# Gate and up projection in seven products per pair of tiles, with streamed down weights

## The chip, the cores and the metric

The kernel runs on one core of one Trainium2 chip. The metric is the device time of one execution in microseconds (us), as the median of several runs. The profiled execution is a separate one; its span goes from the first to the last instruction of the core.

## The reference, cut to what matters

```python
mod = silu(c) @ w_mod                       # six vectors sa, ca, ga, sb, cb, gb of 1024
h = layernorm(x) * (1 + ca) + sa
x = x + ga * attention(h)                   # 32 heads, window of 512 keys, wq [1024, 4096], wo [4096, 1024]
h = layernorm(x) * (1 + cb) + sb
g = silu(h @ w_gate)                        # w_gate, w_up: [1024, 3584]
u = h @ w_up
x = x + gb * ((g * u) @ w_down)             # w_down: [3584, 1024]
```

There are 2048 tokens of 1024 numbers, all bf16. The change is in the last four lines, the feed-forward part.

## The kernel before, in words

A token chunk is 512 tokens, and there are four of them. Tokens lie along the free dimension of the normed input `h_sb[slot]`, which has eight tiles of 128 input features by 512 tokens; slot is the chunk's number modulo 2. The residual `x_sb` stays in SBUF for the whole kernel.

The program runs in this order: opening (conditioning vectors, first layer norm), attention for chunks 0 to 3 of 32 heads each, every chunk followed by its output projection `oproj`, and then the feed-forward part for chunks 0 to 3. The order on each engine is the order in which the Python code emits the instructions; there is no scheduler. A tracker (`T.op`) puts a semaphore wait ahead of an instruction for each buffer that it reads or writes. Small generators in the list `tasks` (layer norm of a later chunk, conditioning vectors) are advanced one step at a time by `run()`, which the main loops call between their own instructions. All bulk transfers are issued by the SP engine, in program order, so a transfer that waits holds up those behind it.

The query projection of the attention already uses seven products instead of eight for a pair of 128-wide heads by two blocks of 256 tokens (`product`, `snap`, `q_add`); its sums of weights (`weight_sums`, L541) and of inputs (`input_sums`) are in fp16.

The feed-forward part before, for each chunk:

- `gateup(ch, ft)` for 28 feature tiles `ft` of 128 columns: 8 matmuls of 128x512 into a gate bank and 8 into an up bank (two banks each, in turn). ScalarE takes tanh(g/2) from the gate bank (L981), VectorE multiplies (t+1)*g (L982) and then times 0.5*u (L984) into `gu`.
- `down(ch, tt, lo, n)` for four token tiles by two halves of the output: 28 matmuls of 128x512 into one of four banks, then `add_to_x` multiplies by the gate vector (L680), adds to `x_sb` (L682), and the row of 128 tokens is stored.

Gate and up weights are loaded in groups of 512 columns (1 MB each, three groups in SBUF), for each chunk anew. The down weights are loaded once, in four parts, and stay. The layer norm of chunk 0 (`ln2[0]`) runs as a task during the attention of chunk 3, the layer norm of chunk n+1 during `gateup` of chunk n.

`oproj(3)` has 256 matmuls of 128x512; 16 of them are done inside the last four heads, then come 48, then 4 blocks of 32, each of which needs one load `load_wo` of 1 MB, then 8 groups of 8 with `add_to_x` behind each.

Of the kernel before, what the change touches and what calls it, by code (L numbers as in the profile page):

```python
# [3 lines left out]
ALU = mybir.AluOpType  # L4
# [4 lines left out]
P = 128  # L9
# [109 lines left out]
def bass_adaLN_cond__sliding_block_cached__swiglu_ffn__prompt_kernel(  # L119
# [28 lines left out]
    FG = FT // 4  # L148
# [104 lines left out]
    Q_last = [dq("q_last%d" % i) for i in range(3)]  # L253
# [6 lines left out]
    with nc.Block() as block:  # L260

        @block.gpsimd
        def _(g):
# [569 lines left out]
            for i in range(NA):  # L833
# [88 lines left out]
            NWG = 3  # L922
            G_AT = [(AT_WQ, AT_WQ + 8), (AT_TQ, AT_TQ + 8), (AT_MS, AT_MS + 8)]
            B_wg, B_wu, wg, wu = [None] * NWG, [None] * NWG, [None] * NWG, [None] * NWG
            Q_wg = [dq("q_wg%d" % i) for i in range(NWG)]
            Q_wu = [dq("q_wu%d" % i) for i in range(NWG)]

            def take_group(s):
                B_wg[s], B_wu[s] = _Buf("wg%d" % s), _Buf("wu%d" % s)
                wg[s] = M.take(G_AT[s][0] * KB, [DT, 512], BF16, [B_wg[s]])  # L930
                wu[s] = M.take(G_AT[s][1] * KB, [DT, 512], BF16, [B_wu[s]])

            def load_gu(gi):
                if gi >= NCH * FG:
                    return
                fg, s = gi % FG, gi % NWG
                for q_, dst, src, b_ in ((Q_wg[s], wg[s], B_w_gate, B_wg[s]), (Q_wu[s], wu[s], B_w_up, B_wu[s])):
                    T.op(q_, lambda: SP.dma_start(dst, src[:, fg * 512:(fg + 1) * 512].rearrange("(k p) n -> p k n", p=P)),
                         writes=[b_])

            take_group(0)
            take_group(1)
            steps = [lambda: None, lambda: load_gu(0), lambda: load_gu(1)]

            def each():
                run(2)
                if steps:
                    steps.pop(0)()

            oproj(NCH - 1, o_list[o_done:], each)  # L950
            finish(ln2[0])
            take_group(2)
            load_gu(2)
            NWD = 4
            B_wd = bufs("wd", NWD)
            wd = M.take(AT_WO * KB, [FT, D], BF16, B_wd)
            Q_wd = [dq("q_wd%d" % i) for i in range(NWD)]
            FW_ = FT // NWD

            def load_wd(i):  # L960
                T.op(Q_wd[i], lambda: SP.dma_start(
                    wd[:, i * FW_:(i + 1) * FW_, :],
                    B_w_down[i * FW_ * P:(i + 1) * FW_ * P, :].rearrange("(f d) n -> d f n", d=P)), writes=[B_wd[i]])

            B_gu = bufs("gu", FT)
            gu = M.take(AT_KT * KB, [FT, CH], BF16, B_gu)
            B_th, B_t1 = bufs("th", 2), bufs("t1", 2)
            th = [M.take((AT_S + i) * KB, [CH], BF16, [B_th[i]]) for i in range(2)]
            t1 = [M.take((AT_S + 2 + i) * KB, [CH], BF16, [B_t1[i]]) for i in range(2)]

            def gateup(ch, ft):
                s = (ch * FG + ft // 4) % NWG
                ff = ft % 4
                gb_, ub_ = ft % 2, 2 + ft % 2
                hs = ch % 2
                for w_, b_, bb in ((wg[s], B_wg[s], gb_), (wu[s], B_wu[s], ub_)):
# [77 lines left out]
```

## Time and profile before

| | us |
|---|---|
| median of 3 runs | 1260.23 (1259.8 to 1261.22) |
| profiled execution, whole | 1259.42 |
| its span | 1257.6 |
| TensorE matmul busy | 1243.1 (99%) |
| VectorE busy | 612.6 (49%) |
| ScalarE busy | 379.0 (30%) |
| feed-forward part, start to the end of the span | about 674.7 to 1257.6 |

The granted TensorE clock is 1.000 of full speed over the whole span. The profile page gives busy time by engine, 40 slices of the span, transfers by queue, the chain of work that ended last, and the costliest groups of instructions by line. An engine's idle time is listed with what released it. Matmul ends are modelled, so the pace of matmuls is read from the distance between what waits for them, or from windows, and not from the mean duration of one.

### The profile page before, as it was taken

How to read it: one execution, taken by the hardware profiler on the slowest of the kernel's cores; microseconds unless marked ns; L12 is line 12 of the kernel's file. 1: busy time of each engine (PE TensorE's matmuls, PEld its weight loads, DVE VectorE, ACT ScalarE, POOL GpSimd, SP SyncE). 2: the span in 40 equal slices, each digit the busy share in tenths (PEclk: the TensorE clock that was granted, in tenths of full speed). 3: DMA queues.
4: the chain of work that ended last, by engine and by line, in shares of the span. 5: the costliest groups of instructions: out<-in, count | busy, mean ns of one | idle time of the engine just before them, and what ended most of it. 6: DMA issues, size and time to landing. Idle time of an engine off the chain costs nothing.

```text
span 1257.6 us, 20341 instructions
## 1 busy us (share of the span) xinstructions
PE 1243.1 (99%) x8298; PEld 709.7 (56%) x8298; DVE 612.6 (49%) x1272; ACT 379.0 (30%) x524; POOL 20.0 (2%) x41
## 2 busy tenths in 40 slices
PE   7999999999999999999999999999999999999999
PEld 4677547876467774688644444444444444444444
DVE  4988318884078860577405543155422543133321
ACT  4677305664046750376500110011100111011100
POOL 1000000000000000000000000000000000000000
PEclk9999999999999999999999999999999999999999
DMA  9999647996469974389267954047420664024200
GB/s 303 255 269 262 215 172 190 269 298 188 149 176 237 260 190 164 95 241 262 50 234 229 338 169 139 20 103 203 139 82 19 161 184 157 25 77 134 67 9 26
DMA packets 235997, 212.49 MB, mean 169 GB/s; under 512 B 106880, under 2 KB 206080, under 8 KB 232064
## 3 DMA queue, kind: packets, MB, share of 16 engines
q1 hardware_dynamic: 235888, 211.19, 59.2%
q8 instruction: 65, 1.06, 0.4%
q14 instruction: 28, 0.23, 0.1%
q10 hardware_dynamic: 16, 0.00, 0.0%
HBM read 174.07 MB, written 12.58 MB: 148 GB/s over the span
## 4 chain that ended last, share of the span: by engine, by line
PE 96%; DVE 1%; SPq 1%; DMA 1%; issue 1%; ACT 0%
PE ps L265 96%; DMA arena<-in_w_mod_dram 1%; SPq L284 1%; DVE arena L670 0%; DVE arena L746 0%; ACT arena L763 0%; DVE arena L602 0%; DMA arena<-arena 0%; DVE arena L636 0%; DVE arena L669 0%; SPq L275 0%; SPq L299 0%; PE ps L269 0%; DVE arena L354 0%; DVE arena L541 0%
## 5 line engine op out<-in xcount | busy, mean ns | idle before, releaser
L265 PE MATMUL ps<-arena 128*128 128x512 bf16 (+4 forms) x8249 | 1239.8, 312 | 8.2 <-DMA arena<-in_w_mod_dram 4.0
L265 PEld LDWEIGHTS ps<-arena 128*128 128x128 bf16 (+1 forms) x8249 | 706.4, 98 | 541.0 <-issue 9.9
L653 ACT ACTIVATE arena<-ps 128x1024 bf16<-128x1024 f32 x256 | 249.7, 1022 | 39.4 <-PE ps L265 36.4
L981 ACT ACTIVATE arena<-ps 128x512 bf16<-128x512 f32 x112 | 66.9, 597 | 518.0 <-PE ps L265 518.0
L680 DVE TENSOR_TENSOR arena<-ps,arena 128x512 bf16<-128x512 f32 (+1 forms) x65 | 44.4, 683 | 339.0 <-PE ps L265 339.0
L982 DVE SCALAR_TENSOR_TENSOR arena<-arena,ps 128x512 bf16<-128x512 bf16 x112 | 76.9, 687 | 141.4 <-ACT arena L981 141.4
L596 ACT ACTIVATE arena<-ps 128x256 f32<-128x256 f32 x134 | 51.3, 383 | 251.4 <-PE ps L265 250.6
L984 DVE SCALAR_TENSOR_TENSOR arena<-arena,ps 128x512 bf16<-128x512 bf16 x112 | 76.9, 687 | 54.5 <-PE ps L265 54.5
L670 DVE TENSOR_TENSOR arena<-ps,arena 128x512 bf16<-128x512 f32 x128 | 88.5, 691 | 4.7 <-DVE arena L669 0.2
L602 DVE TENSOR_TENSOR arena<-ps,arena 128x256 bf16<-128x256 f32 x180 | 75.5, 420 | 11.0 <-PE ps L265 6.3
L669 DVE RECIPROCAL arena<-ps 128x4 f32<-128x4 f32 x128 | 23.0, 180 | 43.3 <-PE ps L265 42.6
L746 DVE SCALAR_TENSOR_TENSOR arena<-arena 128x512 f32<-128x512 bf16 x56 | 41.5, 742 | 0.1
L354 DVE BATCH_NORM_STATS2 arena<-arena 128x6 f32<-128x512 bf16 x60 | 41.1, 685 | 0.1
L361 POOL TENSOR_TENSOR arena<-arena 128x1 f32<-128x1 f32 x30 | 17.5, 583 | 983.4 <-DVE arena L359 980.9
L541 DVE TENSOR_TENSOR arena<-arena 128x1024 f16<-128x1024 bf16 (+1 forms) x48 | 32.4, 682 | 0.2
L636 DVE CAST arena<-ps 128x256 bf16<-128x256 f32 x60 | 25.2, 419 | 10.2 <-PE ps L265 9.0
L682 DVE TENSOR_TENSOR arena<-arena 128x512 bf16<-128x512 bf16 (+1 forms) x65 | 27.3, 420 | 2.2
L598 DVE COPY arena<-ps 128x256 f32<-128x256 f32 x46 | 19.4, 421 | 13.8 <-PE ps L265 13.7
L375 DVE TENSOR_SCALAR arena<-arena 128x512 bf16<-128x512 bf16 x56 | 20.4, 405 | 0.0
L365 DVE TENSOR_SCALAR arena<-arena 128x1024 bf16<-128x1024 bf16 x32 | 17.3, 541 | 2.8 <-DMA arena<-arena 2.5
L269 PE MATMUL ps<-arena 128*128 128x128 bf16 (+1 forms) x49 | 4.9, 262 | 3.6 <-DVE arena L345 3.6
L358 DVE BATCH_NORM_AGGREGATE arena<-arena 128x2 f32<-128x12 f32 x30 | 6.3, 209 | 1.0
(43 smaller groups left out, 51.2 us busy)
## 6 DMA issues: line engine op xcount, KB each, us to landing
arena<-in_A_wq_dram SPq DMA_DIRECT2D x64, 512.0 KB, 4.9
arena<-in_A_wo_dram SPq DMA_DIRECT2D x32, 1024.0 KB, 5.5
arena<-in_B_w_gate_dram SPq DMA_DIRECT2D x28, 1024.0 KB, 5.3
arena<-in_B_w_up_dram SPq DMA_DIRECT2D x28, 1024.0 KB, 7.3
arena<-wq_sums SPq DMA_DIRECT2D x22, 1024.0 KB, 6.3
arena<-in_w_mod_dram SPq DMA_DIRECT2D x8, 1024.0 KB, 7.8
wq_sums<-arena SPq DMA_DIRECT2D x8, 1024.0 KB, 5.6
arena<-in_B_w_down_dram SPq DMA_DIRECT2D x4, 1792.0 KB, 10.5
```

What stands on the lines that cost most here:

```text
L265: T.op(PE, lambda: TE.matmul(out_ap, lhsT, rhs, start=start, stop=stop, skip_group_check=loose), reads=reads, writes=bb)
L354: T.op(DVE, lambda: V.bn_stats(st_sb[i][:, 6 * hf:6 * hf + 6], x_sb[:, t, 512 * hf:512 * hf + 512]), reads=[BX[t]], writes=[B_st[i]])
L541: T.op(st, lambda: e.tensor_tensor(dst, x, y, op), reads=reads, writes=[dst_b])
L596: T.op(ACT, lambda: A.activation(sn[k], bank(QBK, 256), AF.Copy), writes=PB[QBK] + [B_sn[k]])
L602: T.op(DVE, lambda: V.tensor_tensor(dst, bank(XBK, 256, off), sn[k], ALU.add), reads=[B_sn[k]], writes=PB[XBK] + [B_q[i % NQ]])
L653: T.op(ACT, lambda: A.activation(ex[i % NEX][:, kt:kt + 2, :], bank(SCB[kt], 1024).rearrange("p (a b) -> p a b", a=2), AF.Exp, scale=att_s ...
L670: T.op(DVE, lambda: V.tensor_tensor(o_sb[i % NOS].rearrange("p (a b) -> p a b", a=TPC), num, rl_bc, ALU.mult), reads=[B_rl], writes=both + ...
L680: T.op(DVE, lambda: V.tensor_tensor(rt[s][:, 0:n], ps_ap, gate[:, lo:lo + n], ALU.mult), reads=[gate_b], writes=bb + [B_rt[s]])
L746: T.op(DVE, lambda: V.scalar_tensor_tensor(acc, ms[:, kc, :], sc[:, kc:kc + 1], acc, op0=ALU.mult, op1=ALU.add), reads=[B_ms, B_sc, B_acc] ...
L981: T.op(ACT, lambda: A.activation(th[e], bank(gb_), AF.Tanh, scale=0.5), writes=PB[gb_] + [B_th[e]])
L982: T.op(DVE, lambda: V.scalar_tensor_tensor(out=t1[e], in0=th[e], scalar=1.0, in1=bank(gb_), op0=ALU.add, op1=ALU.mult), reads=[B_th[e]], w ...
L984: T.op(DVE, lambda: V.scalar_tensor_tensor(out=gu[:, ft, :], in0=t1[e], scalar=0.5, in1=bank(ub_), op0=ALU.mult, op1=ALU.mult), reads=[B_t ...
```

## The change

Two chunks are taken together as a stretch of 1024 tokens, so the feed-forward part has two stretches. For a pair of feature tiles (256 columns) and a stretch, the weight block is split 2x2 (input features 0 to 511 and 512 to 1023, left and right 128 columns), and the input block 2x2 (input features, first and second chunk). Seven products of 4 matmuls of 128x512 give the four result blocks, in place of 4 blocks of 8 matmuls (Strassen's method in Winograd's form). This holds for gate and for up, so a pair has 14 products, 56 matmuls, in place of 64.

- `sums_of_pair`: VectorE forms four sums of 128x512 of the weights of the next pair, for gate and up, in fp16.
- `stretch_sums`: VectorE forms four sums of the inputs of a stretch, each in two instructions of 128x1024.
- `keep`: products 1, 6 and 5 accumulate in one bank (one for gate, one for up); after each of them ScalarE copies the running total to SBUF in fp32.
- `add`: products 2, 7 and 4 go to banks of their own (4 onto 7), and VectorE adds the kept total to each.
- `silu` on ScalarE uses the Silu function in place of Tanh; `times` multiplies on VectorE, one instruction for each of the four result blocks.
- Weights of a pair are loaded as two transfers of 512 KB (`load_raw`, rows of 512 bytes), three pairs in SBUF.
- `down` runs once for each half of the output and each stretch, with eight banks for eight token tiles at once. Its weights come in blocks of 4 feature tiles by 512 columns (512 KB), six or seven in SBUF, 28 blocks for the two stretches and two halves (one of them twice).
- The layer norm of chunk 1 moves to the end of the attention of chunk 3 and into `oproj(3)`; those of chunks 2 and 3 move into the two down passes of stretch 0. `oproj` calls `each()` also between its first 48 matmuls, which emits the first two weight loads, the Silu table load, the rest of the layer norm and the sums.

```diff
                 for n, a_ in enumerate(first):
                     o_mm(*a_)
+                    if n % 4 == 3:
+                        each()
...
+                if ch == NCH - 1 and h == 28:
+                    finish(ln2[0])
+                    ln2[1] = ln_task(1, g2, B_g2, sb, B_sb)
+                    tasks.append(ln2[1])
...
+            def pair_product(gp, m, n, b):
+                w_, bw = raw[gp % NRW][m], B_raw[gp % NRW][m]
+                ti = (2 * gp + m) % NTS
+                s_i = {3: 3, 5: 0, 6: 1, 7: 2}.get(n)
+                t_i = {4: 3, 5: 0, 6: 1, 7: 2}.get(n)
+                for kc in range(4):
...
+                    mm(bank(b), lhsT, rhs, kc == 0 and n in (1, 2, 7), kc == 3, [lb, hb], PB[b], loose=True)
...
+                def keep(m, n, i):
+                    b = acc_b[m]
+                    pair_product(gp, m, n, b)
+                    T.op(ACT, lambda: A.activation(fn[m][i], bank(b), AF.Copy), writes=PB[b] + [B_fn[m][i]])
+
+                def add(m, n, b, i):
+                    pair_product(gp, m, n, b)
...
+                    T.op(DVE, lambda: V.tensor_tensor(ring[c_], bank(b), fn[m][i], ALU.add),
+                         reads=[B_fn[m][i]], writes=PB[b] + [bs[c_]])
...
+                keep(0, 1, 0)
+                sums_of_pair(gp + 1, 0, 0)
+                g_ = add(0, 2, one[0], 0)
+                keep(1, 1, 0)
+                sl = silu(g_[0], [g_[1]], [])
+                keep(0, 6, 1)
+                sums_of_pair(gp + 1, 0, 1)
+                u_ = add(1, 2, one[1], 0)
+                times(f0, 0, u_, sl)
+                keep(1, 6, 1)
+                sums_of_pair(gp + 1, 0, 2)
+                keep(0, 5, 0)
+                sums_of_pair(gp + 1, 0, 3)
+                g_ = add(0, 7, two[0], 0)
+                keep(1, 5, 0)
+                sl = silu(g_[0], [g_[1]], [])
+                sums_of_pair(gp + 1, 1, 0)
+                u_ = add(1, 7, two[1], 0)
+                times(f1, 1, u_, sl)
+                pair_product(gp, 0, 3, acc_b[0])
+                sl = silu(bank(acc_b[0]), [], PB[acc_b[0]])
+                sums_of_pair(gp + 1, 1, 1)
+                g_ = add(0, 4, two[0], 1)
+                pair_product(gp, 1, 3, acc_b[1])
+                times(f1, 0, (bank(acc_b[1]),), sl, PB[acc_b[1]])
+                sl = silu(g_[0], [g_[1]], [])
+                sums_of_pair(gp + 1, 1, 2)
+                u_ = add(1, 4, two[1], 1)
+                times(f0, 1, u_, sl)
+                sums_of_pair(gp + 1, 1, 3)
+                load_raw(gp + NRW)
...
+                for b_ in range(2):
+                    for k in range(TPS):
+                        for f in range(4 * b_, 4 * b_ + 4):
+                            d_mm(k, f)
+                        each()
+                    load_wd(base + b_ + NWD)
+                for b_ in range(2, FG - 2):
+                    for f in range(4 * b_, 4 * b_ + 4):
+                        for k in range(TPS):
+                            d_mm(k, f)
+                        each()
+                    load_wd(base + b_ + NWD)
+                for k in range(TPS):
+                    for f in range(FT - 8, FT):
+                        d_mm(k, f)
...
+                    done(k, order[k], 0, n, Q_out[k % 4])
+                    each()
```

On ScalarE, the end of the attention and the feed-forward part read as follows before (L653 is the exponential of the attention, L596 a copy of the query projection, L981 the tanh of a feature tile):

```order
L596 ACTIVATE arena<-ps 128x256
L653 ACTIVATE arena<-ps 128x1024 x2
L596 ACTIVATE arena<-ps 128x256
L653 ACTIVATE arena<-ps 128x1024 x8
L981 ACTIVATE arena<-ps 128x512 x112
```

and now (line numbers are those of the changed kernel: L652 is the exponential, L1113 the first use of Silu, L996 the copy in `keep`, L1010 the `silu`):

```order
L652 ACTIVATE arena<-ps 128x1024 x8
L1113 ACT_TABLE_LOAD
L1113 ACTIVATE arena<-arena 128x4
L996 ACTIVATE arena<-ps 128x512 x2
L1010 ACTIVATE arena<-arena 128x512
L996 ACTIVATE arena<-ps 128x512 x4
L1010 ACTIVATE arena<-arena 128x512
L1010 ACTIVATE arena<-ps 128x512
L1010 ACTIVATE arena<-arena 128x512
L996 ACTIVATE arena<-ps 128x512 x2
```

One instruction for a feature tile and chunk has become ten for a pair of tiles and a stretch, six copies and four Silu; the row of the table load stands once.

On VectorE, two feature tiles of chunk 0 read before (L982 and L984 are the two products, L354 to L359 the layer norm of chunk 1):

```order
L354 BN_STATS arena<-arena 128x6
L982 SCALAR_TENSOR_TENSOR arena<-arena,ps 128x512
L984 SCALAR_TENSOR_TENSOR arena<-arena,ps 128x512
L354 BN_STATS arena<-arena 128x6
L358 BN_AGGR arena<-arena 128x2
L359 TENSOR_SCALAR arena<-arena 128x1
```

and the first part of a pair reads now (L540 is a sum of weights, L1003 the `add` from a bank, L1014 the `times`):

```order
L540 TENSOR_TENSOR arena<-arena 128x512
L1003 TENSOR_TENSOR arena<-ps,arena 128x512
L540 TENSOR_TENSOR arena<-arena 128x512
L1003 TENSOR_TENSOR arena<-ps,arena 128x512
L1014 TENSOR_TENSOR arena<-arena 128x512
L540 TENSOR_TENSOR arena<-arena 128x512 x2
L1003 TENSOR_TENSOR arena<-ps,arena 128x512
L540 TENSOR_TENSOR arena<-arena 128x512
L1003 TENSOR_TENSOR arena<-ps,arena 128x512
L1014 TENSOR_TENSOR arena<-arena 128x512
```

The layer norm is gone from between them, and sums of weights stand in its place, ahead of the additions that free the banks.

On SP, behind the last transpose of an attention head (L676), the transfers of `oproj(3)` read before (L503 is a block of `wo`, L938 a group of gate or up weights):

```order
L676 DMA_TRANSPOSE arena<-arena 128x4x128 [waits q_tr3,s_dve]
L503 DMA arena<-in_A_wo_dram 128x4x1024 [waits s_pe,q_wo0]
L503 DMA arena<-in_A_wo_dram 128x4x1024 [waits s_pe,q_wo1]
L503 DMA arena<-in_A_wo_dram 128x4x1024 [waits s_pe,q_wo2]
L503 DMA arena<-in_A_wo_dram 128x4x1024 [waits s_pe,q_wo0]
L938 DMA arena<-in_B_w_gate_dram 128x8x512 [waits q_wq0_1,q_wq0_0]
```

and now (L675 is the head's transpose, L946 `load_raw`, L370 the transposes of the layer norm of chunk 1, L502 `wo`):

```order
L675 DMA_TRANSPOSE arena<-arena 128x4x128 [waits q_tr3,s_dve]
L946 DMA arena<-in_B_w_gate_dram 128x8x256 [waits q_ms1]
L946 DMA arena<-in_B_w_up_dram 128x8x256
L946 DMA arena<-in_B_w_gate_dram 128x8x256 [waits q_ms0]
L946 DMA arena<-in_B_w_up_dram 128x8x256
L370 DMA_TRANSPOSE arena<-arena 128x8x128 [waits s_pe,q_tr0]
L370 DMA_TRANSPOSE arena<-arena 128x8x128 [waits q_tr1,s_dve]
L502 DMA arena<-in_A_wo_dram 128x4x1024 [waits s_pe,q_wo0]
L370 DMA_TRANSPOSE arena<-arena 128x8x128 [waits q_tr2,s_dve]
L370 DMA_TRANSPOSE arena<-arena 128x8x128 [waits q_tr3,s_dve]
L502 DMA arena<-in_A_wo_dram 128x4x1024 [waits s_pe,q_wo1]
```

Four weight loads and two transposes have moved ahead of the first block of `wo`, and two more transposes ahead of the second.

More of the change, by code (lines that the diff above doesn't have):

```diff
@@ L252, in bass_adaLN_cond__sliding_block_cached__swiglu_ffn__prompt_kernel @@
     Q_out = [dq("q_out%d" % i) for i in range(4)]
-    Q_last = [dq("q_last%d" % i) for i in range(3)]
+    Q_last = [dq("q_last%d" % i) for i in range(1)]
     tr_n = [0]
@@ L945, in each @@
[L945 to L963, printed above, removed]
@@ L987, in _ @@
[L987 to L997 removed]
+            NST, NPR, TPS = 2, FT // 2, 2 * TPC
@@ new lines, in _, with each @@
+            warm_s, B_ws = shift, B_shift
+            todo = prepare(True)
+            def each():
+                if len(todo) > 17:
+                    todo.pop(0)()
+                    return
+                for _ in range(2):
+                    if tasks:
+                        run()
+                    elif todo:
+                        todo.pop(0)()
+            oproj(NCH - 1, o_list[o_done:], each)
+            for g_ in list(tasks):
+                finish(g_)
+            while todo:
+                todo.pop(0)()
```

201 lines of the change are left out of this document (131 added, 70 removed).

## The prediction

> **What bounds the kernel now.** I read the page first (busy time, then the chain that ended last), and then the windows of the feed-forward part.
>
> ```profile
> PE 1243.1 (99%) x8298; PEld 709.7 (56%) x8298; DVE 612.6 (49%) x1272; ACT 379.0 (30%) x524; POOL 20.0 (2%) x41
> ...
> PE 96%; DVE 1%; SPq 1%; DMA 1%; issue 1%; ACT 0%
> ```
>
> TensorE is busy for 99% of the span and is 96% of the chain. The windows (length, busy time and instruction count of PE, PEld, DVE, ACT, POOL, then clock, DMA share, GB/s) show gate and up of chunk 0, its down projection, and gate and up of chunk 3:
>
> ```profile
> 674.70:771.30 96.60, 96.60 (x450) 43.81 (x448) 49.60 (x85) 16.72 (x28) 2.19 (x4) 1.00 0.70 219
> 771.30:819.60 48.30, 48.30 (x226) 21.88 (x225) 8.50 (x15) 0.00 (x0) 0.00 (x0) 1.00 0.17 58
> ...
> 1109.50:1206.00 96.50, 96.50 (x449) 43.78 (x448) 38.76 (x57) 16.72 (x28) 0.00 (x0) 1.00 0.28 90
> ```
>
> TensorE never idles there, at full clock, and the other engines are half idle. So in these stages time is the number of matmuls times their pace. The timeline of ScalarE gives the pace, since each tanh waits for its gate bank:
>
> ```profile
> 676.47 0.60 ACT L981 ACTIVATE arena<-ps 128x512 bf16<-128x512 f32 x1 [55.95 <-PE ps L265]
> 679.92 0.60 ACT L981 ACTIVATE arena<-ps 128x512 bf16<-128x512 f32 x1 [2.86 <-PE ps L265]
> ```
>
> 16 matmuls in 3.45 us are 0.2156 us each. The windows agree: 96.6/448 in groups of 8 to a bank, and 48.3/224 in groups of 28. Group length thus costs nothing, and I carry the pace over to groups of 4.
>
> **Part 1: fewer matmuls, -48.3 us.** Gate and up take 28 tiles x 4 chunks x 16 = 1792 matmuls before, and 14 pairs x 2 stretches x 56 = 1568 now. The 224 that go are worth 224 x 0.2156 = 48.3 us, if fp16 weights run at the same pace. Two groups of 256-wide matmuls in the query projection show that they do (busy, mean ns):
>
> ```profile
> L265 PE MATMUL ps<-arena 128*128 128x256 f16 x960 | 134.6, 273 | 0.1
> L265 PE MATMUL ps<-arena 128*128 128x256 bf16 x776 | 107.9, 273 | 2.4 <-ACT arena L763 1.2 <-DVE arena L636 0.6 <-DVE arena L669 0.3
> ```
>
> 134.6/960 = 0.140 us and 107.9/776 = 0.139 us. A pair then takes 56 x 0.2156 = 12.08 us, or 0.863 us for each of its 14 products, as long as the other engines keep up. The down projection keeps its 896 matmuls and its two 256-wide groups at the end, so nothing changes there.
>
> **Part 2: do VectorE and ScalarE keep up? 0 us.** Groups by form, whose durations I use:
>
> ```profile
> L602 DVE TENSOR_TENSOR arena<-ps,arena 128x256 bf16<-128x256 f32 x180 | 75.5, 420 | 11.0 <-PE ps L265 6.3
> L680 DVE TENSOR_TENSOR arena<-ps,arena 128x512 bf16<-128x512 f32 x63 | 43.5, 691 | 334.7 <-PE ps L265 334.7
> L680 DVE TENSOR_TENSOR arena<-ps,arena 128x256 bf16<-128x256 f32 x2 | 0.8, 424 | 4.2 <-PE ps L265 4.2
> L682 DVE TENSOR_TENSOR arena<-arena 128x512 bf16<-128x512 bf16 x63 | 26.7, 424 | 2.1
> L541 DVE TENSOR_TENSOR arena<-arena 128x1024 f16<-128x1024 bf16 x44 | 29.6, 681 | 0.0
> L541 DVE TENSOR_TENSOR arena<-arena 128x1024 f16<-128x1024 f16 x4 | 2.8, 692 | 0.1
> L981 ACT ACTIVATE arena<-ps 128x512 bf16<-128x512 f32 x112 | 66.9, 597 | 518.0 <-PE ps L265 518.0
> L481 ACT ACTIVATE arena<-arena 128x512 bf16<-128x512 bf16 x2 | 1.3, 715 | 1.0 <-DVE arena L419 1.0
> L342 ACT ACT_TABLE_LOAD x1 | 1.3, 1283 | 1.4 <-PEq L1039 1.4
> ```
>
> VectorE for a pair: 6 additions from a bank at 0.691 (L602, the same kind at 256 wide, equals L680 at that width), 8 sums at 0.424 (L541 shows that fp16 output keeps the fast rate: 681 ns for twice the width), 3 products from SBUF at 0.424, one from a bank at 0.691. That is 4.15 + 3.39 + 1.27 + 0.69 = 9.5 us. The timeline shows what lies between two dependent instructions: 0.03 us (674.74 + 0.69 to 675.46), so 18 of them add 0.5.
>
> ```profile
> 674.74 0.69 DVE L680 TENSOR_TENSOR arena<-ps,arena 128x512 bf16<-128x512 f32 x1 [0.58 <-PE ps L265]
> 675.46 0.42 DVE L682 TENSOR_TENSOR arena<-arena 128x512 bf16<-128x512 bf16 x1
> ```
>
> 10.0 of 12.08 us is 83%. An fp16 product with bf16 output is not in the trace; between 0.424 and 0.691 it is nearest to L541, and the upper end would make 10.8, which still fits. ScalarE: six copies and one Silu from a bank at 0.597, three Silu from SBUF at 0.597 to 0.715 make 6.0 to 6.3 us, 52%.
>
> In-order queues can stall TensorE though neither engine is full, so I walk one pair (time from its start, end of product n at n x 0.863). Tightest on ScalarE: the copy of the up total behind product 3 ends at 2.59 + 0.60 = 3.19, the first Silu (its addition ends by 2.9, after the sum ahead of it and the work left over from the pair before) at 3.9, the copy of the gate total behind product 4 at 4.5. Product 7 needs that bank at 5.18: 0.7 us to spare. On VectorE, the addition behind product 8 ends at 7.6 and product 12 needs the bank at 9.49; the one behind product 10 ends at 9.3 against 11.2; the product out of the up bank at 11.9 against 13.8. VectorE ends the pair's list some 1.7 us into the next pair, and makes that up in its first wait, for product 5. So 0 us, with 0.7 us as the smallest margin.
>
> ScalarE's table load of 1.283 us falls into the 55.95 us in which ScalarE idles (row 676.47 above). The order shows one such row for the whole feed-forward part, ahead of all of it: 0 us.
>
> **Part 3: the entry, +0.5 us (0 to 6).** The layer norm of chunk 1, the eight half sums of the stretch and the eight sums of pair 0 now lie on VectorE in `oproj(3)`. VectorE's timeline there:
>
> ```profile
> 662.65 0.69 DVE L680 TENSOR_TENSOR arena<-ps,arena 128x512 bf16<-128x512 f32 x1 [38.81 <-PE ps L265]
> ```
>
> Until this first `add_to_x` it is idle for 38.81 us, against 8 half sums at 0.681, 8 sums at 0.424 (together 8.8) and a layer norm of about 13 us (the window of chunk 0's gate and up has 49.6 - 38.8 = 10.8 more busy time than that of chunk 3, plus waits for transposes). It fits, with the last sums between the `add_to_x`. The layer norms of chunks 2 and 3 go beside down passes, whose window shows VectorE busy 8.50 of 48.30: 0 us.
>
> The transfers are the doubt. SP's own timeline (start, duration) and the landing time of the `wo` blocks (L503), the size of a `w_down` load, and two windows at full transfer rate, the first with gate and up rows of 1 KB, the second with `w_down` rows of 2 KB:
>
> ```profile
> 593.59 31.48 SPq L676 DMA_TRANSPOSE arena<-arena  x11
> 628.16 19.36 SPq L503 DMA_DIRECT2D arena<-in_A_wo_dram  x4
> ...
> 686.87 0.37 SPq L938 DMA_DIRECT2D arena<-in_B_w_gate_dram  x1
> 688.60 0.37 SPq L938 DMA_DIRECT2D arena<-in_B_w_up_dram  x1
> 689.02 3.59 SPq L961 DMA_DIRECT2D arena<-in_B_w_down_dram  x2
> 692.65 8.96 SPq L371 DMA_TRANSPOSE arena<-arena  x1
> ...
> arena<-in_B_w_down_dram SPq DMA_DIRECT2D x4, 1792.0 KB, 10.5
> ...
> DMA to landing us min/median/max: 5.0/5.5/10.9
> ...
> 655.00:660.00 5.00, 5.00 (x25) 2.24 (x23) 0.00 (x0) 0.00 (x0) 0.00 (x0) 1.00 1.08 366
> 698.00:700.00 2.00, 2.00 (x11) 0.88 (x9) 1.52 (x3) 0.00 (x0) 0.00 (x0) 1.00 1.05 387
> ```
>
> The last head's transpose leaves SP at 593.59 + 31.48 = 625.1. Now four weight loads (2.1 MB) and two transposes go ahead of the `wo` block that went out at 628.16. It is needed when TensorE enters the second of its four middle blocks: 674.7 less 64 and 96 matmuls of 0.2156, at 640.2. With 2 KB rows 16 engines move 387 GB/s (84.7 ns a row), with 1 KB rows 366 (44.8 ns); the line through both gives 24.8 ns for 512-byte rows, an estimate of 330 GB/s, and 6.4 us for the four. They are through by about 633.5. A transpose issued onto a full queue can hold SP (8.96 us in row 692.65, behind two loads of 1 MB and two of 1.8), so I put the `wo` block at 632 to 634, landed by 637 to 640: no wait or nearly none. If a 512-byte row costs as much as one of 1 KB (44.8 ns), the loads take 11.5 us, the block goes out at about 639, lands at 644.5, and TensorE waits 4.3 us; one more slow transpose makes 6. I take 0.5, since the line rests on two measured rates.
>
> The Trainium skill, "DMA: Bandwidth & Descriptors", Specifications, puts the smallest transfer for line rate at 512 bytes. By that the four loads take 5.4 us at 387 GB/s, the wait is 0 and the sum 1211.9; the trace has no 512-byte rows to agree or disagree.
>
> **Part 4: streamed weights, 0 us.** A pair needs 1 MB in 12.08 us, 87 GB/s, where the window before had up to 219; its loads go out two pairs (24 us) ahead. A down block of 0.5 MB is needed every 32 x 0.2156 = 6.9 us, and goes out five to six blocks ahead. Landing of 11 us as the worst of L503 is inside both. A down pass begins with the banks that the last pair freed first and reaches the last one 6 us later; between two passes a bank is read within 0.7 us and needed 12 us later.
>
> **The sum.** Profiled execution: 1259.42 - 48.3 + 0.5 = 1211.6. The median of the runs lies 0.81 above the profiled one, so 1212.4 us.
>
> **The rivals.** (B) The first `wo` block is late by 2 us or more: 1214 to 1218 (part 3). For it: the four loads really stand ahead of it, and one transpose held SP for 9 us. Against: needed only 12 us later than it went out before.
>
> (C) VectorE becomes the bound: if the 11 instructions from SBUF alone run at the bank rate, 11 x 0.267 = 2.9 more, 12.9 us of work and some 13.0 a pair; 28 x 0.9 = 25, so about 1237, anything from 1220 to 1245. Against it stand the rows of L541.
>
> (D) Not faster: ScalarE reloads its table at each change between copy and Silu, four in a pair. At 1.283 (L342) the chain at product 7 becomes 3.19 + 1.28 + 0.7 + 1.28 + 0.6 = 7.05 against 5.18: a wait of 1.9 us a pair, 53 us, 1265 in all. It decides from 48.3/28 = 1.73 us a pair on. For it: the functions do alternate. Against it: the order has one load. The Trainium skill, "ScalarE: Activation LUTs", What ACT_TABLE_LOAD costs, gives 2.66 us with its drain for every switch to another set, which would make the wait 4.6 us and the time about 1340; its section on table sets says that cheap functions such as copy are in every set, so that no switch would occur. The trace here shows only the load itself, 1.283.
>
> **How the numbers follow.** My forecast (A, 1211 to 1214) has 0.73, B 0.15, C 0.08, D 0.02, and 0.02 for a time below A. The range 1210.8 to 1217.5 holds A and most of B. 0.2% (2.5 us) is about what a measurement can tell from no change. Only D and the far end of other waits end there or above: faster 0.965, same 0.01, slower 0.025.
>
> **What the changed profile would show.** Part 1: a window over a stretch's gate and up of 14 x 12.08 = 169.1 us in place of 193.2, with TensorE fully busy. Part 2: VectorE about 80% busy and ScalarE about 50% there, no wait of TensorE for either; a wait at product 7 for ScalarE, or at 12 for VectorE, would prove it wrong. Part 3: TensorE idle for a `wo` transfer near 640. Part 4: no wait for `w_down`, gate or up transfers. The prediction fails if a pair takes over 12.3 us or if waits at the entry exceed 5 us.

## The result and the profile after

The changed kernel takes 1212.08 us (median of 4 runs, 1211.85 to 1213.98) against 1260.08 us for the kernel before, run beside it. The ratio is 0.9621, 95% interval 0.9604 to 0.9637. The profiled execution takes 1212.06 us, its span is 1210.3 us, 47.3 us less than before. The first lines of the page and of its chain that ended last:

```profile
PE 1194.9 (99%) x8074; PEld 687.8 (57%) x8074; DVE 712.4 (59%) x1568; ACT 474.5 (39%) x694; POOL 20.1 (2%) x41
...
PE 95%; DMA 2%; DVE 2%; issue 1%; SPq 0%; ACT 0%; POOL 0%; DVEq 0%
```

TensorE has 224 matmuls fewer and is still busy for 99% of the span. VectorE gained 100 us of work and ScalarE 95 us, and neither has taken over the chain. The windows (columns as before) show gate and up of the first and of the second stretch:

```profile
675.70:844.80 169.10, 169.10 (x786) 76.63 (x784) 119.99 (x250) 80.35 (x140) 0.00 (x0) 1.00 0.35 102
...
941.40:1110.50 169.10, 169.10 (x786) 76.63 (x784) 117.83 (x244) 80.34 (x140) 0.00 (x0) 1.00 0.28 80
```

The ends of these windows are chosen; what they show is that TensorE is busy for all of 169.10 us and that 784 weight loads (the second count, one for each matmul of 14 pairs) fall into it. Before, the 896 of two chunks took 193.2. VectorE is busy for 120.0 of 169.1 us (71%), ScalarE for 80.35 (48%). TensorE's waits have one new row (in total, times, longest); before, no matmul waited for a `wo` transfer:

```profile
PE ps L264 <- DMA arena<-in_A_wo_dram: 0.8, 2, 0.4
```

The timelines of TensorE, SP and VectorE at the entry, where `oproj(3)` runs (start, duration, in brackets the idle time ahead and what ended it):

```profile
640.49 7.07 PE L264 MATMUL ps<-arena 128*128 128x512 bf16 x32 [0.37 <-DMA arena<-in_A_wo_dram]
647.95 52.39 PE L264 MATMUL ps<-arena 128*128 128x512 bf16 x242 [0.39 <-DMA arena<-in_A_wo_dram]
...
625.07 0.57 SPq L946 DMA_DIRECT2D arena<-in_B_w_gate_dram  x1
...
627.39 1.51 SPq L946 DMA_DIRECT2D arena<-in_B_w_up_dram  x1
629.00 5.32 SPq L370 DMA_TRANSPOSE arena<-arena  x2
634.41 0.53 SPq L502 DMA_DIRECT2D arena<-in_A_wo_dram  x1
637.55 4.21 SPq L370 DMA_TRANSPOSE arena<-arena  x2
641.85 13.61 SPq L502 DMA_DIRECT2D arena<-in_A_wo_dram  x4
...
636.98 0.55 DVE L364 TENSOR_SCALAR arena<-arena 128x1024 bf16<-128x1024 bf16 x1 [8.45 <-DMA arena<-arena]
```

Two `wo` blocks are late, by 0.37 and 0.39 us. Each wait costs about 0.16 us more than its length: the 32 matmuls between the two take 7.07 us, where 32 x 0.2156 is 6.90. (One matmul alone has 0.379 us in the records, 0.16 more than the pace; that this is the reason is an inference.) Together that is 1.08 us. The last addition of the projection starts at 675.77 instead of 674.74, 1.03 us later. So the account closes: -48.3 + 1.08 = -47.2, against 47.3 between the spans. It closes this well because the two profiled executions leave the last wait of the attention, ahead of anything changed in TensorE's work, at nearly the same time (621.83 before, 621.79 now). The experiments leave it at 621.5 to 623.5, so a difference of 1 or 2 us between two spans need not come from the edit.

### The profile page after: what moved, and what is told of

The parts are those of the page before. It is cut to its first block, busy times and chain, and to the rows that moved or that the text cites. A ratio compares the mean times of both kernels' runs of the same rounds, so it can differ in the third digit from the quotient of the medians.

```text
span 1210.3 us, 20581 instructions
## 1 busy us (share of the span) xinstructions
PE 1194.9 (99%) x8074; PEld 687.8 (57%) x8074; DVE 712.4 (59%) x1568; ACT 474.5 (39%) x694; POOL 20.1 (2%) x41
## 4 chain that ended last, share of the span: by engine, by line
PE 95%; DMA 2%; DVE 2%; issue 1%; SPq 0%; ACT 0%; POOL 0%; DVEq 0%
PE ps L264 95%; DMA arena<-arena 1%; DMA arena<-in_A_wo_dram 0%; DMA arena<-in_w_mod_dram 0%; PE ps L268 0%; DVE arena L669 0%; ACT arena L764 0%; DVE arena L353 0%; DVE arena L601 0%; DVE arena L635 0%; DVE arena L747 0%; SPq L274 0%; DVE arena L668 0%; SPq L370 0%; DVE arena L364 0%
## 5 line engine op out<-in xcount | busy, mean ns | idle before, releaser
L264 PE MATMUL ps<-arena 128*128 128x512 bf16 (+5 forms) x8025 | 1191.4, 310 | 9.2 <-DMA arena<-in_w_mod_dram 4.4
L264 PEld LDWEIGHTS ps<-arena 128*128 128x128 bf16 (+1 forms) x8025 | 684.3, 98 | 515.6 <-issue 11.6
L652 ACT ACTIVATE arena<-ps 128x1024 bf16<-128x1024 f32 x256 | 249.7, 1022 | 39.3 <-PE ps L264 36.4
L996 ACT ACTIVATE arena<-ps 128x512 f32<-128x512 f32 x168 | 100.1, 596 | 283.0 <-PE ps L264 283.0
L1003 DVE TENSOR_TENSOR arena<-ps,arena 128x512 f16<-128x512 f32 x168 | 115.8, 689 | 83.1 <-PE ps L264 80.3
L540 DVE TENSOR_TENSOR arena<-arena 128x512 f16<-128x512 bf16 (+2 forms) x288 | 131.9, 477 | 0.6
L669 DVE TENSOR_TENSOR arena<-ps,arena 128x512 bf16<-128x512 f32 x128 | 88.5, 692 | 4.7 <-DMA arena<-arena 0.2
L1010 ACT ACTIVATE arena<-arena 128x512 f16<-128x512 f16 x84 | 52.5, 625 | 27.8 <-DVE arena L1003 27.8
L1014 DVE TENSOR_TENSOR arena<-arena 128x512 bf16<-128x512 f16 x84 | 35.8, 426 | 9.2 <-DVE arena L1003 0.7
L1014 DVE TENSOR_TENSOR arena<-ps,arena 128x512 bf16<-128x512 f32 x28 | 19.4, 692 | 7.9 <-PE ps L264 7.9
```

What stands on the lines that cost most here:

```text
L264: T.op(PE, lambda: TE.matmul(out_ap, lhsT, rhs, start=start, stop=stop, skip_group_check=loose), reads=reads, writes=bb)
L540: T.op(st, lambda: e.tensor_tensor(dst, x, y, op), reads=reads, writes=[dst_b])
L652: T.op(ACT, lambda: A.activation(ex[i % NEX][:, kt:kt + 2, :], bank(SCB[kt], 1024).rearrange("p (a b) -> p a b", a=2), AF.Exp, scale=att_s ...
L669: T.op(DVE, lambda: V.tensor_tensor(o_sb[i % NOS].rearrange("p (a b) -> p a b", a=TPC), num, rl_bc, ALU.mult), reads=[B_rl], writes=both + ...
L996: T.op(ACT, lambda: A.activation(fn[m][i], bank(b), AF.Copy), writes=PB[b] + [B_fn[m][i]])
L1003: T.op(DVE, lambda: V.tensor_tensor(ring[c_], bank(b), fn[m][i], ALU.add), reads=[B_fn[m][i]], writes=PB[b] + [bs[c_]])
```

## The experiments

All of them are edits of the changed kernel. Times are medians; the kernel before had 1260.16 us beside the first four, 1260.54 beside those with one and three extra Silu, with table loads, and with the weight loads behind `wo`, 1260.96 beside five Silu and the two with the layer norm behind `wo`, and 1259.54 beside the last.

**Eight products, the rest as changed.** Each result block is made in 8 matmuls again, without the copies, the additions and the sums of weights inside the pairs. The stretches, Silu, the streamed weights, the moved layer norms and the sums at the entry stay.

```diff
-                keep(0, 1, 0)
...
-                sums_of_pair(gp + 1, 1, 3)
...
+                for j, (fi, half) in enumerate(((0, 0), (1, 0), (1, 1), (0, 1))):
+                    bg, bu = order[2 * j % 6], order[(2 * j + 1) % 6]
+                    full(0, fi, half, bg)
+                    sl = silu(bank(bg), [], PB[bg])
+                    full(1, fi, half, bu)
+                    times(f0 + fi, half, (bank(bu),), sl, PB[bu])
```

> The changed kernel with gate and up in eight products per pair (64 matmuls) in place of seven; stretches of 1024 tokens, Silu, streamed down weights and the moved layer norms stay. Theory A (the 224 matmuls are the whole gain, all else costs about 1 us at the entry): 1212.1 + 48.3 = 1260.4 us, within 1259 to 1262, and a stretch's gate and up takes 193.2 us. Rival R1 (the other parts of the change gain or cost several us themselves, and part 1 was worth less or more than its count): outside 1257 to 1264.

Measured: 1260.96 us, ratio 1.0007 (0.9997 to 1.0016). The window of the first stretch:

```profile
677.90:871.10 193.20, 192.25 (x879) 87.57 (x896) 39.15 (x57) 33.44 (x56) 0.00 (x0) 1.00 0.31 88
```

The 896 weight loads (the second count) are one for each matmul: 193.2/896 = 0.2156. With 64 matmuls a pair the whole gain is gone, so the stretches, Silu and the streamed weights together gained nothing.

**Gate in seven, up in eight.** Half of the saving; the four sums of the up weights go too.

```diff
-                keep(1, 1, 0)
                 sl = silu(g_[0], [g_[1]], [])
+                up(0, 0, 0, sl)
...
-                keep(1, 6, 1)
                 sums_of_pair(gp + 1, 0, 2)
+                b3 = up_b[1]
+                full(1, 1, 1, b3)
```

> Gate in seven products, up in eight. Theory A (time follows the count of matmuls, no wait between engines): 112 matmuls more than the changed kernel, 112 x 0.2156 = 24.1 us, so 1236.2 us (1235 to 1238). Rival (waits for banks eat part of a saved matmul's worth): the first half of the saving is worth clearly more or less than the second, so 1232 or less, or 1240 or more.

Measured: 1237.61 us, ratio 0.9819 (0.9804 to 0.9833).

```profile
676.80:858.00 181.20, 180.36 (x825) 82.17 (x840) 85.53 (x155) 59.82 (x98) 0.00 (x0) 1.00 0.32 95
```

181.2 us for 840 matmuls is 0.2157 again. 896, 840 and 784 matmuls lie on one line: the gain is matmuls times pace.

**More sums on VectorE.** The first of two kernels forms the four gate sums of each pair twice, the second adds 12 sums a pair.

```diff
                 sums_of_pair(gp + 1, 0, 0)
+                sums_of_pair(gp + 1, 0, 0)
```

> The four gate sums of each pair are formed twice, so VectorE has four more instructions of 128x512 in a pair. Theory A (a pair has 3 us of idle VectorE time in the trace, and the additions that free banks have 1.9 us to spare): no change, 1211.5 to 1213.5 us. Rival C' (VectorE is already at its limit, because it has to be early at each bank): 4 x 0.4 x 28 = 45 us at most, at least 1217.

> The gate sums of each pair are formed three times and the up sums twice, 12 more instructions. Theory A (VectorE is occupied 9.0 us of a pair in the trace; 12 x 0.375 = 4.5 more make 13.5 against TensorE's 12.08): VectorE bounds the pair, 28 x 1.4 = 40 us, so about 1252 us (1240 to 1265), and a stretch's gate and up takes about 189 us. Rival (VectorE's slack is larger than the idle time shows): under 1225.

Measured: 1212.69 us (ratio 0.9622) and 1259.27 us (0.9991, 0.9982 to 1.0). The window of the first stretch with four more sums, then that with twelve more, a row of TensorE's waits and one of ScalarE's:

```profile
676.00:845.00 169.00, 168.26 (x770) 76.62 (x783) 142.44 (x308) 81.36 (x140) 0.00 (x0) 1.00 0.35 103
```

```profile
676.00:868.00 192.00, 169.39 (x765) 74.01 (x778) 181.84 (x413) 78.47 (x139) 0.00 (x0) 1.00 0.31 89
...
PE ps L264 <- ACT arena L996: 41.8, 26, 1.7
...
ACT arena L1010 <- DVE arena L1003: 146.2, 81, 2.5
```

At 84% busy VectorE still costs nothing; with twelve more a pair takes (1257.1 - 1210.3)/28 = 1.67 us longer than in the changed kernel, 13.75, as VectorE's work alone (181.84/14 = 13.0 us) is more than the 12.08 of the matmuls; VectorE is 95% busy (181.84 of 192.0). The waits are put down to ScalarE's copy (L996), but that copy stands in ScalarE's queue behind a Silu that waits for VectorE (146.2 us in all, where the changed kernel has 27.8): the engine named is not the one that is full. So VectorE can become the bound, as rival (C) has it, at a point between 84% and 95% busy, and the changed kernel is at 71%.

**More work on ScalarE, in front of the tightest bank.** One, three and five extra Silu stand behind the first Silu of a pair, ahead of the copy behind product 4.

```diff
                 sl = silu(g_[0], [g_[1]], [])
+                for _ in range(3):
+                    c_ = cnt["sl"] % len(sl_)
+                    T.op(ACT, lambda: A.activation(sl_[c_], g_[0], AF.Silu), reads=[g_[1]], writes=[B_sl[c_]])
```

> One more Silu of 128x512 on ScalarE in each pair, right behind the first Silu, into a buffer that is overwritten later. Theory A (the copy behind product 4 ends 4.19 us into a pair in the trace, and product 7's first matmul could start at about 5.0; the extra one moves the copy by 0.5): no change, 1211.5 to 1213.5 us. Rival (the margin of 0.7 is used up already by latencies between engines): 28 x 0.5 = 14 us, 1226.

> Three more Silu at the same place. Theory A (the copy ends at 4.19 + 1.5 = 5.7 against 5.0, and each wait costs 0.16 more for refilling): 0.86 x 28 = 24 us, 1236 us (1228 to 1244), although ScalarE is busy for only 62 to 65% of a pair. Rival (only the busy share counts, and a third of ScalarE's time is free): 1212.

Measured: 1213.09 us with one (0.9627, 0.9609 to 0.9644), no wait in the stage; 1244.33 us with three (0.9873, 0.9855 to 0.9891). The timeline of the kernel with three, ScalarE and TensorE of one pair, and its window:

```profile
693.01 1.94 ACT L1024 ACTIVATE arena<-arena 128x512 f16<-128x512 f16 x3
694.86 1.06 ACT L996 ACTIVATE arena<-ps 128x512 f32<-128x512 f32 x2
...
695.50 6.86 PE L264 MATMUL ps<-arena 128*128 128x512 f16 x30 [0.94 <-ACT arena L996]
...
676.20:861.00 184.80, 170.87 (x771) 75.58 (x784) 120.09 (x251) 103.56 (x182) 0.00 (x0) 1.00 0.32 93
```

ScalarE is 56% busy and yet TensorE waits in every pair: what counts is its place in the queue, not its share. The three hold the copy (L996) back by 694.86 - 693.01 = 1.85 us, and the wait is 0.94, so the margin was 0.91 us. With one, which holds it back by 0.52 us, there is no wait. The loss is 32 us, not the 24 expected: 0.94 + 0.16 a pair is 1.10, 31 us for 28 pairs.

**Table loads in the pair.** An Exp of four columns ahead of the first Silu makes ScalarE load two tables a pair.

```diff
+                T.op(ACT, lambda: A.activation(warm_s, warm_s, AF.Exp, scale=0.0), reads=[B_ws], writes=[B_ws])
                 sl = silu(g_[0], [g_[1]], [])
```

> One exponential of 128x4 on ScalarE ahead of the first Silu of each pair, so that the table is loaded twice in each pair. Theory A (a load costs 1.283 us, the row of the trace, and nothing behind it): the copy behind product 4 moves by 2 x 1.28 + 0.2 = 2.8 to 7.0 against 5.0, 2.1 us a pair with the refill, 59 us, 1271 us. By the Trainium skill, ScalarE: Activation LUTs, What ACT_TABLE_LOAD costs, a switch is 2.66 us: 4.9 us a pair, about 1349.

Measured: 1294.02 us (1289.7 to 1296.65), ratio 1.0264 (1.0239 to 1.0289). The second load of a pair and the Silu behind it in ScalarE's timeline, TensorE's wait, and the window of a part of the first stretch:

```profile
741.48 1.28 ACT L1010 ACT_TABLE_LOAD   x1
742.77 0.63 ACT L1010 ACTIVATE arena<-arena 128x512 f16<-128x512 f16 x1
...
PE ps L264 <- ACT arena L996: 57.2, 28, 2.0
...
720.00:760.00 40.00, 33.77 (x146) 14.54 (x147) 23.45 (x50) 23.30 (x36) 0.00 (x0) 0.96 0.36 105
```

The waits are 2.04 + 0.16 us a pair, 62 us, about the 59 that loads of 1.283 us give. The spans differ by 82.9; the other 21 us were in no theory. TensorE's timeline has them: behind 12 of the 28 waits the matmuls up to the next wait take 13.95 us, and 12.26 behind the others, and 12 x 1.69 is 20.3. The last window has the mark: clock 0.96, where it is 1.00 in the changed kernel and in the one with three Silu. Either table loads or the length of the wait could have done that.

**Five Silu: the same wait without a table load.**

> Five extra Silu behind the first Silu of each pair, where three were run before; no table load. From the run with three (a wait of 0.94 us in each pair), two more at 0.61 us each make the wait 2.16 us, as long as the wait of 2.04 us in the run with table loads. Theory A (the lower granted clock of that run comes from a wait of this length in every pair): clock 0.94 to 0.96 in the stage, some 20 us on top of the waits, 1290 to 1305. Theory B (it comes from the table loads or that chip's run): clock 1.00, 28 x (2.16 + 0.16) = 65 us over the changed kernel, 1274 to 1280.

Measured: 1305.55 us (1302.24 to 1307.62), ratio 1.0351 (1.0333 to 1.0369), half a us above theory A's range and far from theory B. TensorE's timeline in three pairs, and the windows of 1 us behind a wait:

```profile
715.52 12.26 PE L264 MATMUL ps<-arena 128*128 128x512 f16 x55 [2.27 <-ACT arena L996]
730.05 13.95 PE L264 MATMUL ps<-arena 128*128 128x512 f16 x55 [2.27 <-ACT arena L996]
746.26 12.26 PE L264 MATMUL ps<-arena 128*128 128x512 f16 x55 [2.27 <-ACT arena L996]
...
730.00:731.00 1.00, 0.95 (x5) 0.48 (x6) 0.00 (x0) 0.48 (x1) 0.00 (x0) 1.00 0.00 0
731.00:732.00 1.00, 1.00 (x5) 0.42 (x4) 0.00 (x0) 0.60 (x1) 0.00 (x0) 0.65 0.07 16
732.00:733.00 1.00, 1.00 (x4) 0.30 (x2) 0.43 (x1) 0.00 (x0) 0.00 (x0) 0.50 0.00 0
733.00:734.00 1.00, 1.00 (x4) 0.34 (x3) 0.59 (x2) 0.00 (x0) 0.00 (x0) 0.50 0.00 0
734.00:735.00 1.00, 1.00 (x5) 0.38 (x4) 0.00 (x0) 0.79 (x2) 0.00 (x0) 0.65 0.00 0
```

Behind every second wait, 14 of 28, the clock is at half for 0.7 + 1 + 1 + 0.7 = 3.4 us (a window that is at half for 70% of it reads 0.65), and the matmuls up to the next wait take 13.95 instead of 12.26 us. The sum: 28 waits of 2.27 + 0.18, and 14 times 1.69, are 92.3 us; the spans differ by 93.5. So waits of this length bring the half clock without any table load. Rival (D) left this price out; whether its wait of 1.9 us a pair would have brought it is not measured, since 1.9 lies between waits that did (2.04) and waits that did not (up to 1.7).

**What the entry's 1 us comes from.** Four kernels change the order of the transfers on SP. In the first three the order on VectorE changes with it; only in the last does it stay. The first puts the four weight loads behind the `wo` blocks; the layer norm of chunk 1 then starts two calls of `each()` sooner.

```diff
-                    todo = [lambda: load_raw(0), lambda: load_raw(1),
...
+                    todo = [lambda: T.op(ACT, lambda: A.activation(warm_s, warm_s, AF.Silu), reads=[B_ws], writes=[B_ws])] + todo[0:6] + [
+                        lambda: load_raw(0), lambda: load_raw(1)] + [
...
-                if len(todo) > 17:
+                if len(todo) > 19:
```

> The first four weight loads (pairs 0 and 1) move from the start of the last output projection to behind its third and fourth blocks' loads; six of the eight half sums of the stretch go ahead of them. Theory A (the two waits of TensorE for wo of 0.37 and 0.39 us, with their refill 1.1 in all, come from transfers ahead of the wo blocks): both waits gone, 1211.0 us, a difference within the spread of runs, so the trace decides. Rival (the four transposes of the layer norm hold SP by themselves, since the normed rows have two buffers): at least one of the waits remains.

Measured: 1213.05 us, ratio 0.9624 (0.9609 to 0.9639). SP and TensorE in the timeline:

```profile
625.88 9.82 SPq L370 DMA_TRANSPOSE arena<-arena  x4
635.80 5.54 SPq L502 DMA_DIRECT2D arena<-in_A_wo_dram  x3
...
642.40 21.96 PE L264 MATMUL ps<-arena 128*128 128x512 bf16 x99 [1.50 <-DMA arena<-in_A_wo_dram]
```

Theory A is wrong, and the rival holds: one wait is left, and it is longer. Without the loads ahead of them all four transposes of the layer norm stand in front of the `wo` block, which goes out at 635.80, later than in the changed kernel.

**The layer norm behind the `wo` blocks.** In the next two the weight loads stay early, and the norm of chunk 1 issues nothing until one block, or three, are out (`13` stands for `7` in the second). Norm and sums so come later on VectorE too, with more of them among the additions of the projection; in that the first expectation, which speaks of SP only, is not right.

```diff
             def each():
+                calls[0] += 1
                 if len(todo) > 17:
                     todo.pop(0)()
                     return
-                for _ in range(2):
+                if calls[0] < 7:
+                    return
+                for _ in range(3):
```

> Only the order on SP changes at the entry: the layer norm of chunk 1 issues nothing until the third `wo` block of the last output projection is out, so its four transposes stand behind that block and ahead of the next; the four weight loads stay where the changed kernel has them. Theory A (the transposes, not the weight loads, hold the `wo` blocks): that block leaves SP at 629 to 630 instead of 634.4, the wait of 0.37 us at 640.5 is gone, and the wait at 648 stays or grows (0.3 to 2 us), since all four transposes are now ahead of the next block: 1211.5 to 1213. Theory B (the weight loads fill the DMA engines and so make the block late): the wait at 640.5 stays though the block is issued earlier. 1212 to 1213 as well; the two waits decide, not the time.

> As the run before, but the layer norm of chunk 1 issues nothing until three `wo` blocks are out; its steps then come three at a time. The weight loads stay early. Theory A (the transposes held the `wo` blocks): both waits are gone, and the last addition of the projection ends at about 674.7 instead of 675.8: 1211.0 (1210.5 to 1211.5). Theory B (the weight loads hold them): at least one wait of 0.3 us or more is left at 640 to 648. Rival that undoes the gain: the norm is now so late that the stretch's half sums end behind the projection, and the first product of the first pair waits for VectorE or the transposed chunk by 1 to 4 us: 1212 to 1215.

Measured: 1217.65 us (0.965, 0.9634 to 0.9666) and 1218.74 us (0.9663, 0.9649 to 0.9678), both slower than the changed kernel. SP, TensorE and VectorE with one block ahead, then TensorE's waits with three ahead:

```profile
629.88 1.62 SPq L502 DMA_DIRECT2D arena<-in_A_wo_dram  x1
631.55 13.89 SPq L370 DMA_TRANSPOSE arena<-arena  x4
645.53 15.03 SPq L502 DMA_DIRECT2D arena<-in_A_wo_dram  x4
...
651.67 38.66 PE L264 MATMUL ps<-arena 128*128 128x512 bf16 x169 [3.88 <-DMA arena<-in_A_wo_dram]
...
640.66 0.55 DVE L364 TENSOR_SCALAR arena<-arena 128x1024 bf16<-128x1024 bf16 x1 [11.36 <-DMA arena<-arena]
```

```profile
PE ps L264 <- ACT arena L996: 4.3, 1, 4.3
```

With one block ahead its own wait is gone, as theory A has it, though the loads still stand in front of it. But the transposes now hold SP for 13.89 us and the next block is 3.88 us late, twice the most expected. The third norm, which rewrites one of two normed rows, waits 11.36 us for the transpose that reads it. With three ahead no `wo` block is late, so the transposes did hold them; but the norm comes so late that the half sums push the last additions on VectorE to 681, and the first pair waits 4.3 us. The long waits bring the half clock too: 0.50 at 652 to 654 us in the first, 0.51 at 686 to 688 us in the second.

**Two transposes, one `wo` block, then the loads.** The orders on TensorE and VectorE are those of the changed kernel.

```diff
+                if 3 < calls[0] < 7:
                     return
-                for _ in range(2):
+                if calls[0] == 7:
+                    load_raw(0), load_raw(1)
...
+                    return
+                for _ in range(2 + (calls[0] in (8, 9))):
```

> The changed kernel with one move on SP alone: the four first weight loads stand behind the first two transposes of chunk 1 and the third `wo` block, and still ahead of the other two transposes and the next `wo` block; the orders on TensorE and VectorE are those of the changed kernel. Theory A (what the two waits at the entry come from is that the first transposes land late behind the weight loads, so that the third norm, which needs their rows, and then the next `wo` block are late): the first two transposes land by 631, the third norm no longer waits 8.45 us, the third `wo` block leaves SP at 630 to 632, the next at about 640 instead of 641.85; both waits at 640.5 and 648 are gone, the last addition of the projection ends at 674.7 instead of 675.8, and the time is 1211.0 (1210.6 to 1211.4), ratio about 0.961. Rival: the weight loads now lie ahead of the other two transposes, which last as long on SP as in the run with the norm behind the third block; the next `wo` block leaves SP behind 642 and TensorE waits for it by 0.5 to 4 us: 1212 to 1216.

Measured: 1213.36 us, ratio 0.963 (0.9617 to 0.9643). SP and TensorE:

```profile
625.80 2.92 SPq L370 DMA_TRANSPOSE arena<-arena  x2
628.81 0.53 SPq L502 DMA_DIRECT2D arena<-in_A_wo_dram  x1
...
636.13 6.35 SPq L370 DMA_TRANSPOSE arena<-arena  x2
642.57 13.81 SPq L502 DMA_DIRECT2D arena<-in_A_wo_dram  x4
...
648.87 51.31 PE L264 MATMUL ps<-arena 128*128 128x512 bf16 x232 [1.15 <-DMA arena<-in_A_wo_dram]
```

The first block goes out at 628.81 and its wait is gone; the third norm waits no longer. Still the second block leaves 16.8 us (642.57 - 625.80) after SP turned to this work, exactly as in the changed kernel (641.85 - 625.07), and TensorE waits 1.15 us. This is the rival's outcome. The runs (1212.16 to 1214.36) overlap with those of the changed kernel, so there is no better version here: in four orders a `wo` block or the sums of the stretch came later than their use. Which part of the 16.8 us is SP's own issue and which is full transfer queues stays open; two more normed rows, or smaller transfers, were not tried.

## Why the prediction was right, point by point

- **The sum.** Forecast were 1211.6 us for the profiled execution and 1212.4 for the median; measured are 1212.06 and 1212.08. That the median is so near is luck in part: the entry cost 0.58 us more than forecast, and the 0.81 us between the median and the profiled execution, taken over from the runs before, were 0.02 this time.
- **Part 1, -48.3 us.** Right: 169.1 us a stretch was forecast, 784 matmuls fall into 169.10 us, and the kernels with 896 and 840 matmuls lie on the same line.
- **Part 2, 0 us.** Right, with more room than forecast. ScalarE's 48% is near the 50% forecast; VectorE is at 71% and not 80. The durations held (groups of the changed kernel, count, busy time, mean ns):

```profile
L1003 DVE TENSOR_TENSOR arena<-ps,arena 128x512 f16<-128x512 f32 x168 | 115.8, 689 | 83.1 <-PE ps L264 80.3
L540 DVE TENSOR_TENSOR arena<-arena 128x512 f16<-128x512 bf16 x224 | 88.8, 417 | 0.0
L1014 DVE TENSOR_TENSOR arena<-arena 128x512 bf16<-128x512 f16 x84 | 35.8, 426 | 9.2 <-DVE arena L1003 0.7
```

  The product that was in no trace, fp16 to bf16, takes 426 ns, where 424 was taken. What failed is the 0.03 us between instructions, put in 18 times: that holds between dependent ones. Independent ones overlap; the durations of a pair add up to 9.4 us, and VectorE is busy for 120.0/14 = 8.6 of them:

```profile
1027.59 0.76 DVE L540 TENSOR_TENSOR arena<-arena 128x512 f16<-128x512 bf16 x2
1028.26 0.68 DVE L1003 TENSOR_TENSOR arena<-ps,arena 128x512 f16<-128x512 f32 x1
...
1027.14 0.60 ACT L996 ACTIVATE arena<-ps 128x512 f32<-128x512 f32 x1 [1.23 <-PE ps L264]
...
1029.88 0.59 ACT L996 ACTIVATE arena<-ps 128x512 f32<-128x512 f32 x1
```

  Two sums occupy 1028.26 - 1027.59 = 0.67 us, not 0.83. The copy behind product 4 ends at 1029.88 + 0.59 = 1030.47. Its pair starts at 1026.28 (the copy behind product 1 starts at 1027.14, and a product takes 0.863), so it ends 4.19 us into the pair where 4.5 was forecast, and the margin at product 7 is 1.0 us and not 0.7. The kernel with three Silu gives 0.91.
- **Part 3, +0.5 us.** The place was right (a `wo` transfer near 640), the size was 1.08, inside the 0 to 6. The size is that of one execution: in the eight experiments that leave the entry alone, the waits for `wo` add up to 0.4 to 1.1 us. The first block left SP at 634.41, 0.4 us behind the forecast's 632 to 634; the next left at 641.85, and of that the prediction said nothing. It counted what SP issues, but not that the third norm has to wait for a transpose to read its row (8.45 us of VectorE's idle time, harmless there) and so holds SP, and the `wo` block behind it. That wait stands on the way to the second block, but it isn't the whole cause: in the last experiment it is gone, the loads and the last two transposes (6.35 us) hold SP longer in its place, and the block leaves as late.

  The rate of the weight loads was taken too high, by a reading of the trace: the window 655 to 660 was said to have rows of 1 KB, but only 879 of its 1346 packets are under 2 KB; the others belong to a `wo` block. The packets of the kernel before from 655 to 660 and from 655 to 657 (rows of 1 KB alone), and those of the changed kernel from 629 to 633 (rows of 512 bytes, but for 32):

```profile
DMA packets 1346, 1.83 MB, mean 366 GB/s; under 512 B 24, under 2 KB 879, under 8 KB 1346
DMA packets 688, 0.70 MB, mean 351 GB/s; under 512 B 2, under 2 KB 688, under 8 KB 688
...
DMA packets 2301, 1.16 MB, mean 290 GB/s; under 512 B 32, under 2 KB 2301, under 8 KB 2301
```

  From 351 and 387 GB/s the prediction's own line through both row sizes gives 296 GB/s for rows of 512 bytes; measured are 290, where it took 330. The Trainium skill's rule of line rate from 512 bytes on ("DMA: Bandwidth & Descriptors", Specifications) forecast no wait; this trace does not agree with it, with 290 GB/s against the 387 of 2 KB rows.
- **Part 4, 0 us.** Right: TensorE waits for no gate, up or `w_down` transfer.
- **The rivals.** (B) did not happen: two `wo` blocks are 0.37 and 0.39 us late. The 3.88 us of one experiment came from another order on SP. (C) did not: the sums and products from SBUF kept the fast rate (417 and 426 ns), and VectorE costs nothing up to 84% busy. (D) does not occur: the one load on ScalarE lies at the entry; with a lower clock it could have cost more than was said.

## What to carry to other kernels

Where TensorE is busy all the time, time is matmuls times pace, and a scheme that saves matmuls by extra work elsewhere pays in full as long as each in-order queue reaches its bank in time; check the tightest bank, not the share of busy time. When transfers are moved onto a queue, write down everything between the old and the new place, and for each one what it must wait for itself. A wait of TensorE had up to three prices in these runs: its length, some 0.16 us behind it, and at about 2 us and more often half clock for 3.4 us.

## What the runs showed of the hardware

- Waits of TensorE of 0.94 us (clock 1.00 throughout), 1.50 us and up to 1.7 us left the granted clock at full speed. Waits of 2.04 and 2.27 us, one in every pair, put it at half for 3.4 us behind 12 and 14 of 28, as did single waits of 3.88 and 4.31 us (the two at the very start of the program, 3.58 and 4.38 us, show no lower clock). The Trainium skill, "TensorE: Matmul & The Clock Gate", What's actually happening, has the two speeds and a window of about 3.4 us, which the 3.4 us at 0.50 agree with; it has the clock fall after about 3.4 us of idling, and here 2.04 us are enough at times.
- A table load takes 1.28 us and the next instruction starts right behind it (741.48 + 1.28 to 742.77). The Trainium skill, "ScalarE: Activation LUTs", What ACT_TABLE_LOAD costs, adds a drain to 2.66 us; this trace doesn't show that, and by it the kernel with two loads a pair would have been at about 1349 us instead of 1294.
- Independent instructions of VectorE overlap by some 0.08 us each: two sums of 0.417 us and the step to the next instruction take 0.67 us. A dependent one starts 0.03 us behind the end of the one before (674.74 + 0.69 to 675.46).
- With the queues full, rows of 512 bytes moved at 290 GB/s, rows of 1 KB at 351 and rows of 2 KB at 387.
